# The last dK of a decode-attention gradient, stored as three row sets

## The chip, the cores and the metric

One core of a Trainium2 chip runs the kernel. Times are device microseconds of one execution; a version's time is the median of several runs. A core has TensorE (PE), VectorE (DVE), ScalarE (ACT), GpSimd (POOL) and SyncE (SP), each with an instruction queue of its own, and 16 DMA engines that carry all transfers between the chip's memory and SBUF, whichever queue issues them.

## The reference

A gated mix of two branches on one token (width 640): attention of one query against cached keys and values (32 heads, 4,096 keys, head size 128), and a small MLP. What is computed is the output and its gradient by nine inputs.

```
q = x @ wq                         # 32 heads of 128
scores = q . k_cache * 128**-0.5
p = softmax(scores);  o = p . v_cache
a = o @ wo
h = x @ w1 + b1;  b = (h * tanh(softplus(h))) @ w2
g = sigmoid(sum(x * gate_w))
out = g * a + (1 - g) * b
# returned: out and the gradients by x, k_cache, v_cache, wq, wo, w1, b1, w2, gate_w
```

The gradients by the two caches are as large as the caches: for each head, dV is the outer product of p with a row of 128, and dK the outer product of ds with the scaled q, 4,096 x 128 numbers each. In bf16 a head's K, V, dK and dV are 1 MB each, and 32 heads make 128 MB of the 164 MB that the kernel moves.

## The kernel before, in words

Keys are laid on partitions: partition p of 128 holds 32 consecutive keys, so a head's tile is `[128, 32, 128]`, 8,192 bytes in each partition, and a row of the transfer is one partition's 8,192 bytes on both sides. `dKv[h]` and `dVv[h]` are views of the outputs with that shape.

The order of the work is written out by hand (the pools run under `manual_schedule`). A loop over heads 0 to 30 transposes V and the next K on TensorE (`v_tr`, `k_tr`), computes softmax, and writes the outer products with two VectorE multiplications each into an `o_sb` tile (`outer`, L583) from a pool of four buffers. `out_pair` (L593) then issues the store on SP's queue. `dv_out(h)` and `dk_out(h)` call it for dV and dK; dK of a head is stored in the turn of the next head. SP issues all loads of K, V and weights too, in program order, and the stores of the weight gradients: `f_dwq_st` (L384) for dwq, `f_dwo_st` (L390) for dwo, L775 for db1 (one row), L776 and L777 for dw1.

Head 31 stands behind the loop: its softmax, dK of head 30, the last group's gradients with dwq and dwo, then `dv_out(31)`, then the three short results (`out`, dx and dgate, five rows of 128 each in the tile `fin_rows`), stored by ACT (L888, L890) and POOL (L889), and as the last line of the kernel `dk_out(31)`.

A DMA signals its end on one of eight semaphores that SP's and ACT's transfers take in turn; a transfer that takes a semaphore again waits until the one before it on that semaphore has landed. When everything is issued, SP waits for all of them and the program ends.

Of the kernel before, what the change touches and what calls it, by code (L numbers as in the profile page):

```python
# [16 lines left out]
def kernel(  # L17
# [24 lines left out]
    nc = tc.nc  # L42
    P = 128
    _, H, Sk, Dh = A_k_cache.shape
# [23 lines left out]
    dKv = out_2.rearrange("b h (p j) d -> (b h) p j d", p=P)  # L68
# [513 lines left out]
    def outer(dst, col4, row, a, b):  # L582
        nc.vector.tensor_tensor(  # L583
            dst[:, a:b, :].rearrange("p j (k t) -> p j k t", t=4),
            row.rearrange("p (k t) -> p k t", t=4).unsqueeze(1).to_broadcast([P, b - a, Dh // 4, 4]),
            col4[:, a:b, :].unsqueeze(2).to_broadcast([P, b - a, Dh // 4, 4]), ALU.mult)

    def out_pair(h, dst, col4, row):
        hh = h % G
        t = outs.tile([P, J, Dh], BF16, name="o_sb", tag="o_sb")  # L590
        for a in (0, JH):
            outer(t, col4, row[:, hh * Dh:(hh + 1) * Dh], a, a + JH)
        nc.sync.dma_start(dst[h], t[:])  # L593

    def dv_out(h):
        out_pair(h, dVv, p4s[h], groups[h // G]["do_row"])

    def dk_out(h):
        out_pair(h, dKv, ds4s[h], groups[h // G]["qs_row"])
# [219 lines left out]
    g, h = NG - 1, H - 1  # L819
# [102 lines left out]
```

## Time and profile before

| | |
|---|---|
| median of 3 runs | 405.97 us (405.25 to 406.81) |
| profiled execution | 405.14 us |
| its span, first to last instruction | 403.4 us |
| mean granted TensorE clock | 0.920 |
| busy: PE / DVE / ACT | 306.3 / 312.1 / 224.0 us (76 / 77 / 56%) |
| moved | 164.72 MB, 408 GB/s in the mean |
| SP's queue (q1), share of 16 engines | 97.9% |
| stores of `o_sb` | 64 of 1 MB, 18.6 us from issue to landing (median) |

How to read it: the span is the time between the first and last instruction that the profile holds; the rest of the execution's time lies around it. In the tables by stretch of time, the column before the last is the mean busy share of the 16 DMA engines, and the last is what they moved. PE stands for TensorE's matmuls, PEld for its weight loads, and a name such as SPq for an engine's instruction queue.

### The profile page before, as it was taken

To read this page: it belongs to the slowest core of one execution; us is meant where nothing else is said; L and a number is where in the kernel's file an instruction comes from. 1 tells how busy PE (TensorE), PEld (TensorE's weight loads), DVE (VectorE), ACT (ScalarE), POOL (GpSimd) and SP (SyncE) were. 2 spreads that over 40 slices of the span, in tenths; PEclk is the share of its full clock that TensorE was granted. 3 is DMA by queue.
4 is the path that set the end of the run, shared out by engine and by line. 5 is a ranking of instruction groups with operands and counts; after the bars stand their busy time and mean duration, and the time that the engine had idled before them with its cause. 6 is when DMAs were issued, how large, how long until landed. Compare 5 with 4: busy or idle time off the path is not lost.

```text
span 403.4 us, 10458 instructions
## 1 busy us (share of the span) xinstructions
PE 306.3 (76%) x4278; PEld 242.3 (60%) x4285; DVE 312.1 (77%) x875; ACT 224.0 (56%) x447; POOL 9.9 (2%) x25
## 2 busy tenths in 40 slices
PE   2689999859888996869787788778798794889500
PEld 1477677647677875656675566656686474677300
DVE  3636877958988797998998888669999984996730
ACT  2256566645555564655577574877676363475600
POOL 3000001000000000000000011000000000000000
PEclk9999999998989899998999997989989898699855
DMA  8999999999999999999999999999999999999892
GB/s 296 425 415 423 424 423 412 416 423 423 418 427 425 422 415 426 424 424 425 425 423 424 425 421 425 416 427 424 424 423 425 423 423 425 420 409 417 365 399 86
DMA packets 27380, 164.72 MB, mean 408 GB/s; under 512 B 2884, under 2 KB 3013, under 8 KB 10950
## 3 DMA queue, kind: packets, MB, share of 16 engines
q1 hardware_dynamic: 27026, 164.05, 97.9%
q8 instruction: 33, 0.54, 0.5%
q14 instruction: 13, 0.11, 0.1%
q0 software_dynamic: 256, 0.01, 0.0%
q10 hardware_dynamic: 52, 0.01, 0.0%
HBM read 82.03 MB, written 82.03 MB: 407 GB/s over the span
## 4 chain that ended last, share of the span: by engine, by line
DMA 60%; PE 15%; DVE 14%; ACT 4%; issue 3%; DVEq 0%; SPq 0%; ACTq 0%
DMA out_dram<-o_sb 38%; DMA Vn<-in_A_v_cache_dram 15%; DVE o_sb L583 8%; PE tr L516 6%; DMA wo_g<-in_A_wo_dram 5%; DMA wq_p<-in_A_wq_dram 2%; DVE junk L259 2%; PE od L611 2%; ACT VT L517 2%; PE dqo_ps L624 1%; ACT KT L517 1%; PE q_ps L212 1%; PE S L524 1%; PE h_ps L409 1%; DVE wq_p L379 1%
## 5 line engine op out<-in xcount | busy, mean ns | idle before, releaser
L517 ACT COPY KT<-tr 128x512 f32<-128x512 f32 x128 | 69.2, 588 | 54.7 <-PE tr L516 54.7
L516 PE MATMUL tr<-ident_f,Vn 128*128 128x128 f32 x512 | 83.3, 297 | 18.6 <-DMA Vn<-in_A_v_cache_dram 12.2
L517 ACT COPY VT<-tr 128x512 f32<-128x512 f32 x128 | 72.2, 585 | 38.2 <-PE tr L516 37.1
L583 DVE TENSOR_TENSOR o_sb<-qs_row,ds 128x2048 bf16<-128x2048 bf16 x64 | 75.4, 1220 | 18.9 <-DMA out_dram<-o_sb 18.7
L516 PEld LDWEIGHTS tr<-ident_f,Vn 128*128 128x128 f32 x512 | 62.7, 152 | 34.1 <-ACT VT L517 12.2
L516 PE MATMUL tr<-ident_f,Kn 128*128 128x128 f32 x512 | 75.1, 293 | 8.2 <-DMA Kn<-in_A_k_cache_dram 5.7
L583 DVE TENSOR_TENSOR o_sb<-do_row,p 128x2048 bf16<-128x2048 bf16 x64 | 75.3, 1218 | 0.0
L516 PEld LDWEIGHTS tr<-ident_f,Kn 128*128 128x128 f32 x512 | 59.9, 151 | 11.2 <-DVE ident_f L169 5.7
L618 ACT COPY row_sb<-od 128x512 f32<-128x512 f32 x32 | 18.8, 586 | 39.5 <-PE od L611 39.5
L524 PE MATMUL DP<-doz,VT 128*128 128x32 bf16 x1024 | 36.2, 178 | 2.8
L524 PEld LDWEIGHTS <-KT 128*128 128x128 bf16 x1024 | 33.4, 98 | 6.5 <-ACT KT L517 3.3
L524 PE MATMUL S<-qz,KT 128*128 128x32 bf16 x1024 | 35.6, 179 | 1.9 <-DVE qz L237 0.2
L524 PEld LDWEIGHTS <-VT 128*128 128x128 bf16 x1024 | 32.9, 97 | 6.4 <-ACT VT L517 5.7
L611 PE MATMUL od<-Kn,ds 128*4 128x512 bf16 x256 | 36.1, 407 | 0.0
L611 PE MATMUL od<-Vn,p 128*4 128x512 bf16 x256 | 36.1, 407 | 0.0
L552 DVE TENSOR_REDUCE negM<-mx 128x1 f32<-128x128 f32 x32 | 9.3, 289 | 23.9 <-PE mx L550 22.0
L259 DVE SCALAR_TENSOR_TENSOR junk<-wo_g,da_bc 128x640 bf16<-128x640 bf16 x32 | 26.3, 821 | 0.4
L568 PE MATMUL mx<-zd,ones_f 128*128 128x2 f32 x64 | 11.1, 243 | 18.9 <-DVE pj L564 18.8
L387 ACT ACTIVATE wo_g<-da_bc,o 128x640 bf16<-128x640 bf16 x32 | 24.6, 822 | 0.0
L329 DVE SCALAR_TENSOR_TENSOR junk<-wq_p,dq_bc 128x512 bf16<-128x512 bf16 x35 | 24.1, 687 | 0.5
L624 PE MATMUL dqo_ps<-ident_f,row_sb 128*128 128x128 f32 x128 | 21.7, 295 | 3.1 <-ACT dh_bc L493 1.1
L568 PEld LDWEIGHTS mx<-zd,ones_f 128*128 128x128 f32 x64 | 9.9, 196 | 22.3 <-DVE pj L564 22.0
(169 smaller groups left out, 326.1 us busy)
## 6 DMA issues: line engine op xcount, KB each, us to landing
out_dram<-o_sb SPq DMA_DIRECT2D x64, 1024.0 KB, 18.6
Kn<-in_A_k_cache_dram SPq DMA_DIRECT2D x32, 1024.0 KB, 19.2
Vn<-in_A_v_cache_dram SPq DMA_DIRECT2D x32, 1024.0 KB, 19.3
wo_g<-in_A_wo_dram SPq DMA_DIRECT2D x8, 640.0 KB, 19.7
out_dram<-wo_g SPq DMA_DIRECT2D x8, 640.0 KB, 19.2
wq_p<-in_A_wq_dram SPq DMA_DIRECT2D x2, 1280.0 KB, 8.4
wq_p<-in_A_wq_dram SPq DMA_DIRECT2D x1, 2560.0 KB
out_dram<-wq_p SPq DMA_DIRECT2D x2, 1280.0 KB
```

Of the source, the lines that this page charges most:

```text
L259: nc.vector.scalar_tensor_tensor(junk[:], in0=wos[g][:, hh, :], scalar=1.0, in1=da_bc[:], op0=ALU.mult, op1=ALU.mult, accum_out=gp["do_col ...
L329: nc.vector.scalar_tensor_tensor(junk[:, cs], in0=wqs[g][:, c, cs], scalar=1.0, in1=gp["dq_bc"][:, cs], op0=ALU.mult, op1=ALU.mult, accum_ ...
L387: nc.scalar.activation(wos[g][:, hh, :], da_bc[:], ACT.Copy, scale=groups[g]["o4"][:, hh:hh + 1])
L516: nc.tensor.transpose(tp[:, t, :], words[:, t * P:(t + 1) * P], ident_f[:])
L517: nc.scalar.copy(dst[:, c * (TB // 2):(c + 1) * (TB // 2), :], tp[:])
L524: nc.tensor.matmul(out, lhsT=Tb[:, c, :, par], rhs=z[:, a:a + J], start=(c == 0 and par == 0), stop=(c == J // 2 - 1 and par == 1))
L552: nc.vector.tensor_reduce(negM[:], mx[:, 0:P], axis=AX.X, op=ALU.max, negate=True)
L568: nc.tensor.matmul(mx[:, P:P + 2], lhsT=ones_f[:], rhs=zds[h][:], start=True, stop=True)
L583: nc.vector.tensor_tensor(dst[:, a:b, :].rearrange("p j (k t) -> p j k t", t=4), row.rearrange("p (k t) -> p k t", t=4).unsqueeze(1).to_br ...
L611: nc.tensor.matmul(od4[32 * c:32 * c + 4, :], lhsT=c4[:, 4 * jb:4 * jb + 16].rearrange("p (j t) -> p t j", t=4)[:, 0, :], rhs=N[:, jb:jb + ...
L618: nc.scalar.copy(od_sb[h][:].rearrange("p j d -> p (j d)"), od4[:])
L624: nc.tensor.transpose(od_sb[h][:, j * (P - 1):j * (P - 1) + P], t[:, j, :], ident_f[:])
```

## The change

`out_pair` stores the tile of dK of head 31 with three transfers on SP's queue in place of one: the 49 even rows (partitions) from 0 to 96, the 49 odd rows from 1 to 97, and the 30 rows from 98 to 127. All other stores, the tile, its two multiplications and the place in the order stay.

```diff
         t = outs.tile([P, J, Dh], BF16, name="o_sb", tag="o_sb")
         for a in (0, JH):
             outer(t, col4, row[:, hh * Dh:(hh + 1) * Dh], a, a + JH)
-        nc.sync.dma_start(dst[h], t[:])
+        if h == H - 1 and dst is dKv:
+            for a, z, s in LAST:
+                nc.sync.dma_start(dst[h][a:z:s], t[a:z:s])
+        else:
+            nc.sync.dma_start(dst[h], t[:])
+
+    LAST = [(0, 98, 2), (1, 98, 2), (98, P, 1)]
```

## The prediction

> **What bounds the kernel now.** I read the page's 40 slices first, then its rows of DMA queues, then the issues on SP's queue in order of time, then a table of the last 15 us. The slices:
>
> ```profile
> DMA  8999999999999999999999999999999999999892
> GB/s 296 425 415 423 424 423 412 416 423 423 418 427 425 422 415 426 424 424 425 425 423 424 425 421 425 416 427 424 424 423 425 423 423 425 420 409 417 365 399 86
> ```
>
> The DMA engines are busy nine tenths of nearly every slice, at some 420 GB/s: the kernel is bound by its transfers. In the last slice that ends: a mean share of two tenths, 86 GB/s. The last dK leaves in this slice, so that is where the change has to be priced. SP's issues just before it (start, duration, line, transfer):
>
> ```profile
> 373.01 0.31 SPq L775 DMA_DIRECT2D out_dram<-dh_bc  x1
> 375.68 0.40 SPq L776 DMA_DIRECT2D out_dram<-w_sb  x1
> 378.23 0.38 SPq L777 DMA_DIRECT2D out_dram<-w_sb  x1
> 379.87 0.35 SPq L593 DMA_DIRECT2D out_dram<-o_sb  x1
> 382.51 0.37 SPq L384 DMA_DIRECT2D out_dram<-wq_p  x1
> 385.01 0.34 SPq L390 DMA_DIRECT2D out_dram<-wo_g  x1
> 389.13 1.65 SPq L593 DMA_DIRECT2D out_dram<-o_sb  x2
> ```
>
> The last row holds two issues, dV and dK of head 31; the answer for this tile has the second at 390.4. Compute is over by then: the last `outer` starts at 385.3 and takes 1.22 us. From 390.4 nothing but transfers is left. The table of the end (DVE, ACT and POOL idle; the last two columns are the share of 16 DMA engines and GB/s):
>
> ```profile
> 390.50:392.50 2.00, 0.00 (x0) 0.00 (x0) 0.00 (x0) 0.00 (x0) 0.00 (x0) 0.50 0.97 401
> 392.50:395.00 2.50, 0.00 (x0) 0.00 (x0) 0.00 (x0) 0.00 (x0) 0.00 (x0) 0.50 1.00 415
> 395.80:397.20 1.40, 0.00 (x0) 0.00 (x0) 0.00 (x0) 0.00 (x0) 0.00 (x0) 0.50 0.06 26
> 397.22:399.66 2.44, 0.00 (x0) 0.00 (x0) 0.00 (x0) 0.00 (x0) 0.00 (x0) 0.50 0.06 24
> 399.68:402.12 2.44, 0.00 (x0) 0.00 (x0) 0.00 (x0) 0.00 (x0) 0.00 (x0) 0.50 0.06 24
> 402.20:403.40 1.20, 0.00 (x0) 0.00 (x0) 0.00 (x0) 0.00 (x0) 0.00 (x0) 0.50 0.00 0
> ```
>
> This decides the case. All 16 engines run until 395.0; from 395.8 to 402.1 the share is 0.06, which is 1/16: **one engine alone**, some 7 us late, sets the end. The trace's records of single packets (start, duration, bytes, queue) give its order: 8 packets of 5,120 bytes (dwo) until 397.21, 8 of 8,192 bytes (dV 31, one row each) until 399.67, 8 of 8,192 (dK 31) until 402.12, with a 4-byte completion after each eight. A row costs it 306 ns from start to start, a completion 6 ns. Then 1.24 us of closing waits and barrier to the span's end, and 1.7 us outside it (405.14 less 403.4).
>
> So the question is not how fast 1 MB goes, but **how many of the last dK's 128 rows fall to the late engine**. Now it has 8.
>
> **Who is the late engine?** The rows of the queues:
>
> ```profile
> q1 hardware_dynamic: 27026, 164.05, 97.9%
> q10 hardware_dynamic: 52, 0.01, 0.0%
> ```
>
> q10 is ACT's. It carries three loads of five rows, one load of one row and the two stores of `fin_rows` with five rows each. If five rows go to five engines, each with its own completion, and one row to one, that is 3x(5+5) + (1+1) + 2x(5+5) = 52, the row to the packet. So a transfer is spread over as many engines as share its rows evenly, at most 16: 128 rows over 16 with eight each, 64 over 16 with four (the last rows of dW2), 5 over 5. The packet records then show that the late engine is one of the five. From 385.5 on only one chain of 3,456-byte packets (dW1) is left, the late engine's, for the others have gone on to dwq and dwo. Both `fin_rows` stores of ACT sit inside that chain; the first:
>
> ```
> start us  took ns  bytes  queue
> 388.242   148      3456   q1
> 388.387    18       256   q10
> 388.401   141      3456   q1
> 388.539     9         4   q10
> 388.545   140      3456   q1
> ```
>
> Each starts 3 to 4 ns before the one ahead of it ends, as one engine's packets do all over the trace.
>
> **The change, part by part.** Compute, loads, pools and every earlier transfer keep their places; only SP's last issue becomes three.
>
> *Rows.* 49 = 7x7, so the even rows go to seven engines with seven rows each, and so do the odd rows; 30 rows go to 15 engines with two each. If the sets are nested (the smaller is part of the larger), the late engine, being one of the five, is one of the seven both times, and of the 15. It gets 7 + 7 + 2 = 16 rows in place of 8: 8 x 306 ns = 2.45 us, and two more completions of 6 ns: **+2.46 us**, wholly on the path, since nothing runs beside this engine at the end. The bounds from both sides: shared evenly by 16 the rows cost about nothing; if the late engine were outside the seven it would keep two rows (-6 x 306 ns = -1.84 us) or none (-2.45 us). I take the upper value, by the rows of ACT's stores.
>
> [...]
>
> *The other 15 engines.* They finish dV 31 at about 395.0 - 2.45 = 392.6. The other six of the seven then need 16 rows, 4.9 us, until 397.5: covered by the late engine, which would end at 402.12 + 2.46 = 404.58. The rest end by 393.2. If the late engine were on time, the seven would end 2.45 us later than all 16 do now: the loss doesn't hang on its lateness.
>
> *SP.* Two more issues of 0.34 us behind the one at 390.4. In the built program part one waits for the second `fin_rows` store, as the single store does now. Parts two and three wait for the transfers that last used their semaphores: L776's, which landed 12.5 us after its issue at 375.7, so before 389, and L775's one row, which was issued before it. All three are out by about 391.5; the late engine comes to them at 399.67. Cost: nothing. That cover would be gone only if they left 8 us later. Behind them SP has only its closing waits; no other engine waits for them, and no buffer is taken again.
>
> *What may be gained.* Nothing starts earlier: part one is issued where the whole store was.
>
> Sum: 405.14 + 2.46 = 407.60 us on the profiled execution. That lies 0.83 us below the median of the runs (405.97), so the forecast is 405.97 + 2.46 = **408.4 us**.
>
> **The rivals.**
>
> *The late engine is outside the seven (ends faster).* The split then takes work off it: two rows left give 405.97 - 1.84 = 404.1 us, none 403.5 us. The other engines' 397.5 would stay below its end (400.3 or 399.7). It decides if the engine sets aren't nested, so that a seven can miss a member of a five, or if another engine is late in the runs that are timed. Against it stands that both ACT stores, one after the other, hit the late engine; for it, that one execution is all I have, and no view shows why this engine is late.
> [...]
>
> *The rows are spread over 16 after all.* 49 rows as three or four each, 30 as one or two: the late engine gets 7 to 10 rows, the time stays within 0.6 us of 405.97. Against it: every transfer I could count was shared evenly.
>
> *The crowded seven slow each other.* If their rows took double, the other six would be at it until about 392.6 + 9.8 = 402.4, and the late engine, which starts dK at 399.67, would lose half of 2.7 us: 408.4 + 1.4 = 409.8 us. Between 393 and 395, with all 16 at work, 8,192-byte packets took 309 to 339 ns; nothing near double.
>
> **How the numbers follow.** The forecast gets 0.78, the late engine outside the seven 0.15, spread over 16 0.05, the crowded seven 0.02. A measurement of this kernel can tell about 0.5% from no change, 2.03 us. The forecast's 2.46 us lies 0.43 us beyond it; the three runs span 1.56 us, so a little of its chance falls short: 0.71 slower, 0.07 same. Of the first rival only the case without rows (-2.45 us) is past the bound: 0.10 faster, 0.05 same. Together: faster 0.10, same 0.17, slower 0.73. The range leaves out the first rival and the crowded seven, 0.17. It reaches down to 405.5, just below the unchanged median, for the even spread, and up to 409.6, the forecast with the upper spread of the runs (406.81 - 405.97 = 0.84) and a little crowding. The forecast's own range is 407.6 to 409.3.
>
> **What would show it.** The packets of q1: the single store is 128 + 16 completions, the three 128 + 7 + 7 + 15, so 27026 becomes 27039; spread over 16 it would be 27058. In the table of the end: a DMA share near 7/16 (0.44) from about 393.2 to 397.5, then 0.06 until about 404.6; a span near 405.8. Sixteen 8,192-byte packets behind dV's eight in the last chain, as seven, seven and two. I am wrong if the engine that ends last has no or two such rows, or if more than seven engines work after 394.

## The result and the profile after

The changed kernel is slower: 411.93 us (median of 6 runs, 411.28 to 413.45) against 405.86 us (6 runs). The ratio is 1.0152, with a 95% interval from 1.0134 to 1.0170: +6.07 us where +2.46 was forecast. The way was right, the size was not, and the time lies above the range.

The page after, its 40 slices of DMA share and GB/s and two rows of its queues:

```profile
DMA  8999999999999999999999999999999999998960
GB/s 280 428 414 424 424 420 421 408 417 414 423 422 427 421 419 422 423 426 423 424 424 425 423 424 423 421 423 425 424 423 425 421 426 425 413 423 372 411 239 26
...
q1 hardware_dynamic: 27039, 164.05, 96.8%
...
q10 hardware_dynamic: 52, 0.01, 0.0%
```

q1 has 27039 packets, the number forecast for engine sets of 7, 7 and 15. The body of the kernel is as before; the last two slices (20 us) are not. SP's last issues, in order of time:

```profile
389.21 0.34 SPq L597 DMA_DIRECT2D out_dram<-o_sb  x1
390.68 5.71 SPq L595 DMA_DIRECT2D out_dram<-o_sb  x3
```

dV leaves at the old time. The three parts of dK take 5.71 us to issue, and all are out by 396.4. The table of the end (the columns as in the prediction: DMA share and GB/s last):

```profile
390.50:392.50 2.00, 0.00 (x0) 0.00 (x0) 0.00 (x0) 0.00 (x0) 0.00 (x0) 0.50 1.00 413
392.50:395.00 2.50, 0.00 (x0) 0.00 (x0) 0.00 (x0) 0.00 (x0) 0.00 (x0) 0.50 0.50 143
395.80:397.20 1.40, 0.00 (x0) 0.00 (x0) 0.00 (x0) 0.00 (x0) 0.00 (x0) 0.50 0.65 178
397.20:399.70 2.50, 0.00 (x0) 0.00 (x0) 0.00 (x0) 0.00 (x0) 0.00 (x0) 0.50 0.43 139
399.70:402.10 2.40, 0.00 (x0) 0.00 (x0) 0.00 (x0) 0.00 (x0) 0.00 (x0) 0.50 0.11 38
402.10:405.00 2.90, 0.00 (x0) 0.00 (x0) 0.00 (x0) 0.00 (x0) 0.00 (x0) 0.50 0.06 23
405.00:407.80 2.80, 0.00 (x0) 0.00 (x0) 0.00 (x0) 0.00 (x0) 0.00 (x0) 0.50 0.06 23
407.80:409.40 1.60, 0.00 (x0) 0.00 (x0) 0.00 (x0) 0.00 (x0) 0.00 (x0) 0.50 0.00 0
```

Three things are to be seen. From 395.8 to 397.2 a share of 0.65 of 16 engines moves only 178 GB/s, where 0.65 of the full 420 would be some 273; from 392.5 to 395.0 a share of 0.50 moves 143 in place of 210. The packets take about half as long again as they would at the full rate. Next, the third part comes late: by the packet records seven engines are busy from 394.0 to 396.5, but 14 to 15 from 397.0 to 398.0, after SP's third issue has ended. And one engine alone works until 407.8, not 404.6.

Read by the records of single packets, the late engine's chain says where the 6.04 us of span went. It ends dwq at 395.75 (before: 395.67). Its eight dwo packets of 5,120 bytes then take 426, 371, 375, 380, 366, 505, 502 and 461 ns in place of 196 each: +1.9 us. dV takes 3.37 us in place of 2.45. dK has seven, seven and two rows, 5.10 us in place of 2.45. From its last completion to the span's end it is 1.62 us in place of 1.24.

### The profile page after: what moved, and what is told of

Same layout as the page of the kernel before. It is cut to its first block, busy times and chain, and to the rows that moved or that the text cites. A ratio compares the mean times of both kernels' runs of the same rounds, so it can differ in the third digit from the quotient of the medians.

```text
span 409.4 us, 10467 instructions
## 1 busy us (share of the span) xinstructions
PE 307.2 (75%) x4285; PEld 242.7 (59%) x4285; DVE 311.8 (76%) x875; ACT 224.2 (55%) x447; POOL 9.9 (2%) x25
## 3 DMA queue, kind: packets, MB, share of 16 engines
q1 hardware_dynamic: 27039, 164.05, 96.8%
## 4 chain that ended last, share of the span: by engine, by line
DMA 48%; DVE 19%; PE 17%; ACT 6%; issue 4%; DVEq 0%; SPq 0%; ACTq 0%
DMA out_dram<-o_sb 41%; DVE o_sb L583 10%; PE tr L516 7%; DMA Vn<-in_A_v_cache_dram 5%; PE od L617 2%; DMA wq_p<-in_A_wq_dram 2%; ACT VT L517 2%; ACT KT L517 2%; PE dqo_ps L630 1%; DVE junk L259 1%; PE S L524 1%; DVE junk L329 1%; PE q_ps L212 1%; DVE mjunk L498 1%; DVE wq_p L379 1%
```

## The experiments

The theories:

- **Rows alone** (the forecast): the late engine's eight more rows, 2.46 us.
- **Shared reads**: the other six of the seven read the tile's partitions across each other, and across the partitions that the late engine still reads for dwo and dV.
- **Strided writes**: every second 8 KB of the destination is slow to write.
- **Issue**: SP is slow to issue a transfer that goes to few engines.

The main readings, all from the late engine's chain in one profile of each kernel, in us (its dwo, its dV, its part of dK, and from its last completion to the span's end), with the ratio of times to the kernel before, which had medians of 405.54 to 405.92 us in these series:

| kernel | dwo | dV | dK (rows) | end | ratio (95%) |
|---|---|---|---|---|---|
| before | 1.55 | 2.45 | 2.45 (8) | 1.24 | 1 |
| the change | 3.44 | 3.37 | 5.10 (16) | 1.62 | 1.0152 (1.0134 to 1.0170) |
| the change again | 3.22 | 3.55 | 5.13 (16) | 1.62 | one run |
| even and odd, 64 rows each | 1.55 | 2.45 | 2.46 (8) | 1.70 | 1.0000 (0.9986 to 1.0014) |
| contiguous 49, 49, 30 | 1.79 | 2.83 | 5.05 (16) | 1.61 | 1.0080 (1.0058 to 1.0102) |
| reads of 64 to 112 | 1.55 | 2.45 | 4.91 (16) | 1.61 | 1.0068 (1.0042 to 1.0094) |
| reads of 52 to 100 | 1.55 | 2.45 | 4.91 (16) | 1.61 | 1.0068 (1.0049 to 1.0087) |
| reads of 15 to 63 | 3.04 | 3.06 | 4.91 (16) | 1.68 | 1.0128 (1.0097 to 1.0159) |
| strided reads, contiguous writes | 3.21 | 3.49 | 5.10 (16) | 1.61 | 1.0153 (1.0123 to 1.0183) |
| contiguous reads, strided writes | 1.79 | 2.83 | 5.05 (16) | 1.61 | 1.0085 (1.0059 to 1.0111) |

**Which engine is late.** dK in six transfers of 112, 6, 4, 3, 2 and 1 rows:

```diff
-    LAST = [(0, 98, 2), (1, 98, 2), (98, P, 1)]
+    LAST = [(0, 112, 1), (112, 118, 1), (118, 122, 1), (122, 125, 1), (125, 127, 1), (127, 128, 1)]
```

> dK 31 in six contiguous transfers of 112, 6, 4, 3, 2 and 1 rows. If a transfer takes the engines counted from the first, as many as divide its rows, they go to 16, 6, 4, 3, 2 and 1 engines, and the late engine's last chain tells its number: seven rows, and then as many single rows as there are transfers it is part of: five for the first engine, four for the second, three for the third, two for the fourth, one for the fifth or sixth, none for a later one. From the two five-row stores I expect one to four (it lacks db1's row, so not the first). Packets of q1: 27026 - 144 + 128 + 16 + 6 + 4 + 3 + 2 + 1 = 27042. Rows alone: 8 to 11 rows, so 405.9 to 406.8 us. Shared reads or strided writes: hardly more, since only 16 rows cross. Issue (slow issues on fewer engines): up to 2 us more, if the late engine waits for them.

It measured 407.0 us, a ratio of 1.0025 (1.0011 to 1.0039). The row of SP's queue:

```profile
q1 hardware_dynamic: 27042, 164.05, 97.6%
```

27042, as counted. The late engine's chain ends with seven rows, a completion, one row, a completion: it takes part in the transfer of six rows and in none of four or fewer. With nested sets it is the fifth or the sixth engine, and since it carries both five-row stores, the fifth. The steps of the forecast on the engines held. It has eight rows as before; the 1 us by which this kernel is slower is about the sum of a closing that is 0.50 us longer (1.74) and of three slow rows in dV and dK (336, 604 and 479 ns, 0.49 us too much).

**The split without fewer engines.** The stride of two, but 64 rows each:

```diff
-    LAST = [(0, 98, 2), (1, 98, 2), (98, P, 1)]
+    LAST = [(0, P, 2), (1, P, 2)]
```

> dK 31 in two transfers, the 64 even rows and the 64 odd rows, so with the stride of the change but all 16 engines and the late engine's eight rows as before (four and four). Rows alone: 405.9 us, no change. Shared reads: the rows that an engine reads are no longer those it reads for dwo and dV, so the late engine meets others in its partitions from about 393 to 398: 406.5 to 408.5 us, less than the 3.6 us that the change loses beyond its rows, because the others need only 8 rows each. Strided writes: about the same, 406.5 to 408.5, but the packets of dwo stay at 196 ns. Issue: 405.9 us, both issues near 0.35 us.

No change, 1.0000. Two rows of its table of the end:

```profile
392.50:395.00 2.50, 0.00 (x0) 0.00 (x0) 0.00 (x0) 0.00 (x0) 0.00 (x0) 0.50 1.01 422
...
399.70:402.10 2.40, 0.00 (x0) 0.00 (x0) 0.00 (x0) 0.00 (x0) 0.00 (x0) 0.50 0.06 27
```

A full share moves 422 GB/s here, and no packet of 8,192 bytes after 390.5 took over 400 ns (in the change 35 did, up to 1,959 ns). So neither the stride nor a second transfer slows a packet by itself when the parts have 64 rows; the closing is 0.46 us longer, which the ratio doesn't tell from nothing (medians 406.19 and 405.56 us). My expectation of 406.5 or more by shared reads was a miss: I had supposed that 64 strided rows would cross, and no packet shows it.

**Contiguous parts.** The change's counts without its stride:

```diff
-    LAST = [(0, 98, 2), (1, 98, 2), (98, P, 1)]
+    LAST = [(0, 49, 1), (49, 98, 1), (98, P, 1)]
```

> dK 31 again in three transfers of 49, 49 and 30 rows, but each a contiguous block of partitions (0 to 48, 49 to 97, 98 to 127), so the engines' row counts stay as in the change (late engine 16 rows) and only the stride of two goes, in SBUF and in the destination. Four theories of what the change costs beyond the late engine's eight more rows (2.46 us of the 6.07 measured). Rows alone: about 408.3 us here. Shared reads (the other six of the seven read partitions that the late engine still reads for dwo and dV, and slow it): contiguous blocks still cross its partitions, so 410 to 414 us, with late-engine packets of dwo (5,120 bytes) well above 196 ns. Strided writes (every second 8 KB of the destination is slow): near 408.5 us. Issue (SP needs longer for a transfer on fewer than 16 engines: the three issues took 5.71 us in the changed kernel): as the change, 411.9 us.

1.0080: about half of the change's loss, and the late engine lost 0.24 us in dwo where the change lost 1.9. At 409.43 us it lay below the 410 to 414 that I had set for shared reads. That looked like the strided writes, or like reads that cross at another time.

**Reads that leave the late engine alone, and reads that hit it.** Destinations and counts stay; only the partitions read by the two 49-row parts move, to begin in turn at 64, 52 and 15, so these rows of dK hold other rows' values:

```diff
-            for a, z, s in LAST:
-                nc.sync.dma_start(dst[h][a:z:s], t[a:z:s])
+            nc.sync.dma_start(dst[h][0:98:2], t[64:113])
+            nc.sync.dma_start(dst[h][1:98:2], t[64:113])
+            nc.sync.dma_start(dst[h][98:P], t[98:P])
```

> As the change in destinations, row counts and engines, but both 49-row transfers read the tile's partitions 64 to 112 (so those 98 output rows of dK 31 hold other rows' values): the first seven engines read nothing from partitions 0 to 63 for them. Rows alone: 408.3 us. Shared reads: if the late engine, one of the first five, reads dwo and dV from partitions below 64, nobody crosses it any more, its dwo packets are back at 196 ns, dV ends near 399.7 us of the span, and the time is 408.3 us; the six may slow each other without setting the end. Strided writes: the destinations are those of the change, so 411.9 us. Issue: 411.9 us.

> As the run that read partitions 64 to 112 for both 49-row transfers, but reading 52 to 100 (those 98 output rows of dK 31 hold other rows' values). The probe with 6, 4, 3, 2 and 1 rows gave the late engine one row of the six and none of the four, so it is the fifth or sixth engine, and with ACT's five-row stores the fifth. Theory A, shared reads at the late engine's own partitions: only reads of the few partitions that it reads itself slow it. [...] Theory B, any reads below partition 64 slow it: between 408.6 and 411.9 us with dwo packets above 196 ns.

> [...] If neither holds: 408.6 us and packets at 196 ns.

With 64 to 112 and with 52 to 100 the late engine is untouched: every dwo packet 196 ns, every row 309 ns with a step of 306, dV at its old 2.45 us. The end of the second, cut at the last completion:

```profile
400.00:405.46 5.46, 0.00 (x0) 0.00 (x0) 0.00 (x0) 0.00 (x0) 0.00 (x0) 0.50 0.06 26
405.46:407.07 1.61, 0.00 (x0) 0.00 (x0) 0.00 (x0) 0.00 (x0) 0.00 (x0) 0.50 0.00 0
```

One engine works its sixteen rows at full rate and ends; what is left over the forecast is the longer closing. With 15 to 63 dwo takes 3.04 us (packets up to 752 ns) and the ratio is 1.0128. In all three the six crowd each other (36 to 52 packets over 400 ns), and where they leave the late engine alone that costs nothing. The last two runs differ in nothing but the partitions read: SP's issues took 0.30, 1.15 and 0.96 us in the one and 0.30, 1.12 and 0.99 us in the other, so issue isn't what parts them. In the probe the six issues took 5.85 us, and the late engine waited for none. So the late engine loses its time to reads of some partitions between 15 and 51; that these are the ones it reads itself is the explanation that fits, and isn't shown: no view gives the partitions that one engine reads, and the runs don't narrow them further.

**Reads or writes.** The stride of the reads with contiguous destinations, and the reverse:

```diff
+            nc.sync.dma_start(dst[h][0:49], t[0:98:2])      # reads strided
+            nc.sync.dma_start(dst[h][49:98], t[1:98:2])
...
+            nc.sync.dma_start(dst[h][0:98:2], t[0:49])      # writes strided
+            nc.sync.dma_start(dst[h][1:98:2], t[49:98])
```

> The change's reads (49 even, 49 odd partitions, 30 more) with contiguous destinations (rows 0 to 48 and 49 to 97 of the output, so those 98 rows of dK 31 are permuted). It differs from the change only in where it writes and from the contiguous version (0 to 48, 49 to 97; +0.8%) only in what is read when. [...] If the stride in the reads makes the crossing fall into dwo and dV: 411.5 to 412 us, dwo packets of the late engine near 400 ns. If the strided writes slow the six so that they cross later: 408.8 to 409.5 us, as the contiguous version.

> The counterpart: contiguous reads (partitions 0 to 48, 49 to 97) into the change's destinations (even and odd output rows; 98 rows of dK 31 permuted). Reads decide: 408.8 to 409.5 us, as the contiguous version, with the late engine's dwo within 0.5 us of 1.55 us. Writes decide: 411.5 to 412 us. In between for both: the two act together.

Strided reads give the whole loss, 1.0153; strided writes give the contiguous version's, 1.0085. Writes cost nothing that shows. Both splits read the same 98 partitions; with contiguous reads the late engine meets two or three slow dwo packets and is through, with strided ones all eight are slow, in the change from 395.8 to 399.2. That the two differ in when they cross is argued, not shown, for something else goes with the stride of the reads. SP's three issues, strided reads first:

```profile
391.35 0.83 SPq L594 DMA_DIRECT2D out_dram<-o_sb  x1
392.23 0.74 SPq L595 DMA_DIRECT2D out_dram<-o_sb  x1
393.03 3.86 SPq L596 DMA_DIRECT2D out_dram<-o_sb  x1
...
390.38 0.30 SPq L594 DMA_DIRECT2D out_dram<-o_sb  x1
390.74 1.07 SPq L595 DMA_DIRECT2D out_dram<-o_sb  x1
391.86 1.00 SPq L596 DMA_DIRECT2D out_dram<-o_sb  x1
```

The issue of the third part took 3.7 to 4.0 us in all three profiles with strided reads and 1.0 to 1.4 us in those with 49, 49 and 30 contiguous ones. So with strided reads its rows, on 15 engines, fall into the middle of dwo; with contiguous ones most or all of them were through before. In the change dwo was slow ahead of them already: three packets of 371 to 426 ns began before the third part's first rows at 396.9, and the five behind took 366 to 505 ns. With the reads of 64 to 112 some 11 engines still worked in dwo's first half microsecond, and it wasn't slowed. But no run has strided reads without the late third part, so what each adds isn't shown apart.

**The change again.**

> The changed kernel once more, for a second profile. In the first, the late engine's eight dwo packets took 366 to 505 ns in place of 196 and dV ended 3.0 us late, and three packets were slow (1,119, 440 and 373 ns) after all other engines had stopped. Shared reads: slow dwo packets again, dV's end 2.5 to 3.5 us later than without crossing (3,200 ns of dwq plus 1,547 of dwo plus 2,450 of dV). If the lone slow packets belong to the change they are here too; if they are a chance disturbance they are gone or elsewhere, and the time is up to 1 us less.

410.95 us in one run, with 405.54 for the kernel before. The slow dwo packets are back (308 to 571 ns), and so are the lone ones after the other engines have stopped: 375, 1,093, 506 and 335 ns (first: 378, 1,119, 440, 373). So these aren't chance. The run with strided reads and contiguous writes has them too (382, 1,119, 440, 373), the contiguous version and the one with contiguous reads have 373, 596 and 449, the reads of 15 to 63 have 469 and 752, and the probe's three were of this kind. They belong to the pattern of the reads, some 1.1 us in the change and 0.5 us in the contiguous versions, and are absent with the reads of 52 to 100 and 64 to 112 and with the 64 even and odd rows. What they wait for when no other engine has a packet on record stays open.

**The closing waits.** The reads of 52 to 100 again, with ACT's two short stores moved to POOL's queue:

```diff
-    nc.scalar.dma_start(out0_rows, fin_rows[0:RC, :])
+    nc.gpsimd.dma_start(out0_rows, fin_rows[0:RC, :])
...
-    nc.scalar.dma_start(out9_rows, fin_rows[2 * RC:3 * RC, :])
+    nc.gpsimd.dma_start(out9_rows, fin_rows[2 * RC:3 * RC, :])
```

> As the run that reads partitions 52 to 100 (98 output rows of dK 31 hold other rows' values), with the two five-row stores of ACT moved to POOL's queue. That takes them out of the turn of the eight semaphores, so the last three transfers come to lie on the sixth, seventh and eighth in the order in which SP waits at the end, in place of the eighth, first and second. Theory: in the change the transfer that lands last is second in that order, so SP has six more waits to run through, 62 ns each, 0.37 us; here it is the last, and the time from the last completion to the span's end falls from 1.61 us to 1.24 us as in the kernel before. Rival: the 0.37 us comes from a transfer on fewer than 16 engines landing later; then it stays 1.6 us.

Its table, cut at the last completion:

```profile
400.00:406.08 6.08, 0.00 (x0) 0.00 (x0) 0.00 (x0) 0.00 (x0) 0.00 (x0) 0.50 0.06 26
406.08:407.38 1.30, 0.00 (x0) 0.00 (x0) 0.00 (x0) 0.00 (x0) 0.00 (x0) 0.50 0.00 0
```

1.30 us in place of 1.61, with the same transfers of dK; 1.24 was expected. The order of the waits accounts for it: SP's records show seven of them, some 62 ns apart, behind the late landing with the reads of 52 to 100, and one here. Its single run took 409.15 us, no less than the 408.84 without this step, since dwq ended 0.6 us later in this profile.

**Versions that take rows off the late engine.** Since it is the fifth, a transfer on four or three engines misses it:

```diff
+    LAST = [(0, 60, 1), (60, P, 1)]                          # both by SP
...
+            nc.gpsimd.dma_start(dst[h][0:77], t[0:77])       # POOL and SP
+            nc.sync.dma_start(dst[h][77:P], t[77:P])
...
+            nc.gpsimd.dma_start(dst[h][0:60], t[0:60])       # POOL and SP
+            nc.sync.dma_start(dst[h][60:P], t[60:P])
```

> Two contiguous transfers on SP, 60 rows (15 engines, four each) and 68 rows (four engines, 17 each): the late engine, the fifth, keeps four of its eight rows, and the first four engines, which wait for it anyway, take 21 each, until about 392.6 + 6.4 = 399.0 us of the span. Rows alone: -4 x 306 ns = -1.22 us, 404.4 us. SP's closing waits stay as before if the 60 rows, on the last of the eight semaphores in the closing order, land last. Shared reads: the 60 rows cross the late engine's partitions while it writes dwq and dwo; if that costs 1 us or more the gain is gone, 405.5 us and over; if the four engines slow each other by half, they end near 402 and set the end, also 405.5.

> A version meant to beat both: the first 77 rows of dK 31 are stored by POOL's queue, the last 51 by SP, on three engines with 17 rows each if the rule of divisors holds. POOL's five-row store put 16 completions into the trace, so its queue spreads rows otherwise than SP's. If 77 rows go to 16 engines with five each, the late engine keeps five rows (-0.92 us); if to eleven consecutive engines with seven each, it keeps seven (-0.31 us) or none (-2.45 us), depending on where they start. By rows alone 403.2 to 405.3 us. [...] The three engines end near 398, if they don't slow each other.

> 60 rows of dK 31 by POOL's queue (four on each of 15 engines, by the way the 77 rows were spread: five each) and 68 by SP on four engines, 17 each. The late engine has four rows for dK in place of eight (five with 77 and 51). Rows alone: -1.22 us, 404.5 us, a little less than with 77 and 51 rows (-0.92 us by rows, -1.3 us measured). If the four engines slow each other as in the kernel with 60 and 68 rows both by SP, they set the end: 404.4 to 405.5 us.

60 and 68 rows by SP: 405.53 us, 0.9993 (0.9978 to 1.0008), nothing. The late engine is done at 401.16, but the four engines, slowed by each other as the expectation feared, end at 401.99 (399.0 was the estimate by rows alone) and set the end. 77 rows by POOL and 51 by SP: **404.36 us, 0.9968 (0.9951 to 0.9985)**, 0.3% below the kernel before. 60 by POOL and 68 by SP: 404.57 us, 0.9980 (0.9965 to 0.9994). Three rows of the better one's DMA table:

```profile
out_dram<-o_sb POOLq DMA_DIRECT2D x1, 616.0 KB, 7.7
out_dram<-o_sb SPq DMA_DIRECT2D x1, 408.0 KB
...
q0 software_dynamic: 352, 0.64, 0.6%
```

POOL's part lands 7.7 us after its issue at 386.7, well ahead of the late engine's end, because its queue isn't behind the late dwq and dwo: the engines take its rows in between. With 60 rows exactly four of them stand in the late engine's chain, before its dwq. Its last completion is then dV's, at 401.06 with 77 rows and 400.88 with 60, where the kernel before ended at 402.13. The three engines are done at 400.84, and the four at 400.97, a little behind the late one, so there seems little more to be had this way.

## Why the prediction was wrong in size

- **Who ends, and the number of rows**: right. One engine sets the end, it is in the seven, and it gets sixteen rows, as seven, seven and two. Where nothing disturbs it they take 4.91 us in place of 2.45, the forecast's +2.46 to the hundredth.
- **The other 15 engines ("covered by the late engine")**: this is the step that failed. I costed their 4.9 us of reads at nothing because they end before the late engine does. But it is on the path while they run, with dwo and dV, and their reads slow it: 1.9 us in dwo. Another 0.96 us in dV with the gap behind it and 0.2 us in dK come with the same reads, but nearly all of that (1.1 us) is the lone slow rows after the others have stopped, whose cause is open. Reads of 52 and up bring all of these to zero. I also had the engines without a 49-row part done by 393.2; with the third part late, eight of them work until about 398.2, and a sign against me that I had named, more than seven engines after 394, came true.
- **The rival of the crowded seven**: right in kind, wrong in place and price. I let only dK's rows be slowed, from 399.7 on, and took my measure of crowding from 309 to 339 ns in transfers of 128 rows, where each engine has its own rows. That row of the trace couldn't show crossing. The split's packets took up to 1,959 ns, and the last of the six was done at 401.1, not at 397.5. It deserved much more than 0.02, and my 409.8 us for it was too low.
- **SP ("Cost: nothing")**: right in that the late engine never waited for an issue, though all three were out at 396.4 and not at 391.5. Whether the third part, being late, added to dwo's loss isn't shown. Wrong for the end: the three parts move the last landing from the last wait in SP's order to the second, +0.38 us.
- **The sum**: 0.08 (dwq's end) + 1.95 (dwo with the gap ahead of it) + 0.96 (dV) + 2.66 (dK: 2.46 and 0.2) + 0.39 (closing) = 6.04 us, the difference of the spans, 409.40 - 403.36.
- **The rivals of no change and of a gain**: both fell with the 27039 packets and the probe.

## What to carry to other kernels

Before splitting a last transfer, find the engine that ends last and count the rows that the split gives it; here a number of rows with a poor divisor was gathered on few engines, 49 on seven (by the 27039 packets of q1), and the late one had sixteen rows in place of eight. Work that ends earlier than the critical engine isn't free for that reason: here the same number of rows lengthened dwo by 1.5 us or not at all, by which partitions they were read from. Ask not only when it ends but what it touches meanwhile. And look at the order in which the program waits at its end: the transfer that lands last should be the last one waited for (here 1.30 us of closing in place of 1.61).

## What the runs showed of the hardware

- Two parts of 64 strided rows didn't crowd at all (no packet of 8,192 bytes over 400 ns after 390.5), while every other split did, also with contiguous rows (21 to 52 such packets). Few engines aren't needed for it: of POOL's 77 rows, some 14 of them under way at once, 38 took over 400 ns.
- A lone engine on the reads of the change had single rows of 1,093 to 1,119 ns after all others had stopped; the cause is open.
- The engines took POOL's rows between those of SP's queue, not behind them: four of the 60 stand in the late engine's chain among dK of head 30, whose transfer SP had issued earlier.
- SP's issue of a transfer took 0.34 us for 128 rows, 0.73 to 0.84 us for 49 strided ones, 0.30 to 1.28 us for 49 contiguous ones, and for the 30 rows behind them 3.7 to 4.0 or 1.0 to 1.4 us. What makes it long is open.
